# Loading x and two small weights at the start of a fused attention and MLP kernel in another order and from other queues

## The chip, the cores and the metric

The kernel runs on one core of a Trainium2 chip. The metric is device time in microseconds of one execution; the median of three runs before the change is 721.4 us (720.83 to 721.46). One further execution was taken by the profiler; every number of the trace comes from it.

## The reference

The kernel computes a transformer block whose attention and MLP work side by side on the same normalised input, for 2048 tokens of width 512, in bf16. Attention has 32 query heads of 16 channels and one key and value head that all of them share.

```
xn = layernorm(x)                                   # 2048 x 512, no gain, no bias
q  = xn @ wq -> 32 heads of 16;  k = xn @ wk;  v = xn @ wv     # wk, wv: 512 x 16
o  = softmax(q k^T / 4) v ;  A = concat(o) @ wo
B  = gelu_tanh(xn @ w1 + b1) @ w2 + b2              # 1792 hidden
out = x + A + B
```

## The kernel before, in words

**Two parts.** The first 24 us are a prologue: x is loaded, normalised, transposed, and K, V and the first queries are projected. From then to the end runs the attention loop: ScalarE computes exponentials (line 1110), VectorE computes others in integer arithmetic (lines 1141, 1162, 1194) with help of GpSimd (line 1161), TensorE computes scores (line 1086) and the products with V (line 1154), and the query projections, MLP and output products (lines 763 and 767) are put between them.

**Order.** All instructions are recorded through `add`, each with what it reads and writes, and a list scheduler (`schedule`) then fixes each engine's order for good; `emit` adds the semaphore waits. At run time each engine executes its own list in order. In the prologue the order of the engines' instructions follows the table `PRO_DUE`, that of DMAs their own due numbers.

**Tiles and pieces.** x has 16 row tiles of 128 rows by 512 (128 KB each), loaded as eight pieces: piece i holds tiles 2i and 2i+1 (256 KB, two rows of 1 KB on each of 128 partitions). Lines 775 to 778 issue them: piece 1 from ScalarE's queue, piece 0 and then 2 to 7 from SyncE's. Lines 779 and 780 issue wk and wv (16 KB each, in rows of 32 bytes) from ScalarE's queue behind piece 1; lines 781 to 783 issue wq, w1 and w2 from SyncE's queue behind piece 7. wo follows (line 1035). Each DMA has a semaphore of its own; whoever reads the data first waits for that.

**Normalising.** `ln_batch` takes the statistics of a tile. For 14 tiles VectorE does this: bn_stats (line 858) and bn_aggr (line 872). For tiles 1 and 4 ScalarE does it in two passes over the tile: a sum (line 855) and, after GpSimd has made the negative mean (line 861), a sum of squares (line 865). ScalarE makes the reciprocal deviation by Ln and Exp (lines 877 and 879). `normed` scales the tile on GpSimd or VectorE (line 895) or ScalarE (line 891), `x_T` transposes it on TensorE (line 914) and copies it back (lines 919 and 921). VectorE takes the tiles' statistics in the order 0, 5, 2, 7, 3, 8, 12, 9, 15, 6, 13, 10, 14, 11, that is the pieces in the order 0, 2, 1, 3, 4, 6, 7, 5. The first use of wk is a copy on GpSimd (line 810), that of wv the V projection on TensorE (line 743, `wvk` as an operand), and that of wq a copy on GpSimd (line 985). TensorE's products with zeros (line 1522) are fillers that keep it busy.

Of the kernel before, what the change touches and what calls it, by code (L numbers as in the profile page):

```python
# [10 lines left out]
P = 128  # L11
# [106 lines left out]
TBW = 512  # L118
# [495 lines left out]
def bass_parallel_sum__grouped_kv_mqa__dense_activation_gelu__prompt_kernel(  # L614
# [33 lines left out]
    with ExitStack() as es:  # L648
# [82 lines left out]
        def dve(fn, r=(), w=(), n=TBW, mode=1, allow=1.0, **kw):  # L731
            return add("dve", fn, r, w, occ=vcost(n, mode), lat=dlat[0], allow=allow, **kw)

        def act(fn, r=(), w=(), n=TBW, allow=0.0, lat=0.22, **kw):
            return add("act", fn, r, w, occ=0.051 + n / 1.2e3, lat=lat, allow=allow, **kw)
# [35 lines left out]
        def dma(eng, o, i, stream, r=(), w=(), lat=2.2, allow=1.0, **kw):  # L771
            return add(eng, lambda e: e.dma_start(o, i), r, w, dma=stream, occ=0.7, lat=lat, allow=allow, **kw)
# [8 lines left out]
        dma("sp", wq_sb[:], A_wq.rearrange("(k p) n -> p k n", p=P), "d_wq", w=["wq"], due=0.4, lat=9.4)  # L781
        dma("sp", w1_sb[:], B_w1.rearrange("(k p) n -> p k n", p=P), "d_w1", w=["w1"], due=0.5, lat=10.4)
        dma("sp", w2_sb[:], B_w2.rearrange("(k p) n -> p k n", p=P), "d_w2", w=["w2"], due=0.7, lat=16.4)
# [57 lines left out]
        def land(ti):  # L841
            return LAND[ti // 2] + 0.2 * (ti % 2)

        col, batch_of = {}, {}

        def ln_batch(ts, how):
            c0, n = len(col), len(ts)
# [4 lines left out]
            for ti in ts:  # L852
                c = col[ti]
                if how == "a":
                    act(lambda e, ti=ti, c=c: e.activation(scr, x_sb[:, ti, :], ACT.Identity, accum_out=sm[:, c:c + 1]),
                        r=[("x", ti)], w=["scr", ("sm", ti)], n=TBW + 320, lat=0.3)
                else:
                    dve(lambda e, ti=ti, c=c: e.bn_stats(stats[:, c, :], x_sb[:, ti, :]), r=[("x", ti)], w=[("st", ti)],  # L858
                        n=511)
# [133 lines left out]
        for _, _, kind, a in sorted(steps, key=lambda s: s[:2]):  # L993
            if kind == "ln":
                ln_batch(list(a[0]), a[1])
            elif kind == "tr":
                x_T(list(range(*a[0])), a[1], a[2])
            elif kind == "k":
                k_proj(list(range(*a[0])), a[1])
            elif kind == "v":  # L1000
                v_tiles(range(*a))
                if a[1] in (NVA, NT):
                    k_max(0 if a[1] == NVA else NVA, a[1])
            else:
# [559 lines left out]
```

## Time and profile before

| what | us |
|---|---|
| median of three runs | 721.4 (720.83 to 721.46) |
| profiled execution, its own time | 720.62 |
| its span, first to last instruction | 718.8 |
| outside the span | 1.8 |
| first exponential of the loop starts (ScalarE, line 1110) | 24.42 |
| busy share of the span: PE, ACT, DVE, POOL | 98%, 98%, 97%, 63% |

PE is TensorE, ACT ScalarE, DVE VectorE, POOL GpSimd, SP SyncE. Times inside the profile count from the start of the span. A DMA appears twice: as the instruction that issues it on its engine's sequencer (SPq, ACTq), and as time to landing, from the start of that instruction to the last signal of its semaphore. q1 is the queue of SyncE's DMAs, q10 that of ScalarE's; both run on the same 16 DMA engines.

### The profile page before, as it was taken

To read this page: it belongs to the slowest core of one execution; us is meant where nothing else is said; L and a number is where in the kernel's file an instruction comes from. 1 tells how busy PE (TensorE), PEld (TensorE's weight loads), DVE (VectorE), ACT (ScalarE), POOL (GpSimd) and SP (SyncE) were. 2 spreads that over 40 slices of the span, in tenths; PEclk is the share of its full clock that TensorE was granted. 3 is DMA by queue.
4 is the path that set the end of the run, shared out by engine and by line. 5 is a ranking of instruction groups with operands and counts; after the bars stand their busy time and mean duration, and the time that the engine had idled before them with its cause. 6 is when DMAs were issued, how large, how long until landed. Compare 5 with 4: busy or idle time off the path is not lost.

```text
span 718.8 us, 22616 instructions
## 1 busy us (share of the span) xinstructions
PE 704.6 (98%) x9221; PEld 219.2 (30%) x9224; DVE 699.1 (97%) x1387; ACT 703.8 (98%) x762; POOL 452.2 (63%) x739
## 2 busy tenths in 40 slices
PE   7999999999999999999999999999999999999998
PEld 5332232222243333223222232222233222222233
DVE  8899999999999999999999999999999999999986
ACT  7899999999999999999999999999999999999997
POOL 8456557786733446787777636676775786767531
PEclk9999999999999999999999999999999999999999
DMA  9200100101010010010101110100100111101111
GB/s 307 81 10 17 33 10 11 32 16 26 9 41 25 24 33 17 14 28 22 39 7 26 47 40 17 29 17 15 24 18 17 25 32 18 39 21 28 27 30 41
DMA packets 36254, 23.59 MB, mean 33 GB/s; under 512 B 17768, under 2 KB 32568, under 8 KB 36152
## 3 DMA queue, kind: packets, MB, share of 16 engines
q1 hardware_dynamic: 34824, 21.86, 12.1%
q8 instruction: 74, 1.21, 0.7%
q10 hardware_dynamic: 1328, 0.30, 0.2%
q14 instruction: 28, 0.23, 0.1%
HBM read 13.28 MB, written 2.35 MB: 22 GB/s over the span
## 4 chain that ended last, share of the span: by engine, by line
ACT 52%; PE 42%; DVE 5%; DMA 1%; issue 0%; SPq 0%
ACT E L1110 49%; PE pAll L1154 21%; PE pAll L1086 13%; PE pAll L767 6%; PE pAll L749 2%; DVE Dt L1141 2%; ACT ub L1343 1%; DVE stats L858 1%; ACT x_sb L1348 1%; DMA x_sb<-in_A_x_dram 1%; DVE Dt L1194 1%; DVE Dt L1162 0%; PE pAll L914 0%; ACT x_sb L1343 0%; PE pAll L1522 0%
## 5 line engine op out<-in xcount | busy, mean ns | idle before, releaser
L1110 ACT ACTIVATE E<-pAll 128x1024 bf16<-128x1024 f32 (+2 forms) x676 | 652.2, 1146 | 2.9 <-PE pAll L1086 1.2
L1161 POOL INT64_ADD Dt<-Dt x671 | 429.9, 649 | 246.0 <-DVE Dt L1141 79.6
L1141 DVE TENSOR_SCALAR Dt<-pAll 128x512 int16<-128x512 f32 (+1 forms) x599 | 412.5, 706 | 6.5 <-PE pAll L763 4.4
L1154 PE MATMUL pAll<-Dt,V 128*32 128x512 bf16 x3120 | 417.1, 383 | 0.0
L1154 PE MATMUL pAll<-E,V 128*32 128x512 bf16 x1424 | 284.5, 385 | 0.5 <-DVE Of L1240 0.4
L1086 PE MATMUL pAll<-QT,KT 32*128 32x512 bf16 x2048 | 266.7, 384 | 5.5 <-ACT E L1110 4.2
L1194 DVE TENSOR_SCALAR Dt<-Dt 128x1024 int16<-128x1024 int16 (+7 forms) x291 | 160.9, 563 | 2.2 <-PE pAll L1154 1.9
L1086 PEld LDWEIGHTS pAll<-QT,KT 32*128 32x128 bf16 x2048 | 66.5, 90 | 276.5 <-ACT E L1110 260.9
L1154 PEld LDWEIGHTS pAll<-Dt,V 128*32 128x32 bf16 x3120 | 106.8, 94 | 115.4 <-issue 79.5
L1162 DVE TENSOR_SCALAR Dt<-Dt 128x1024 int16<-128x1024 int16 (+1 forms) x270 | 90.0, 360 | 0.1
L1154 PEld LDWEIGHTS pAll<-E,V 128*32 128x32 bf16 x1424 | 65.7, 94 | 49.1 <-issue 38.5
L767 PE MATMUL pAll<-xnT,w_sb 128*32 128x512 bf16 x520 | 70.5, 382 | 0.0
L767 PE MATMUL pAll<-w_sb,ub 128*32 128x512 bf16 x364 | 49.4, 381 | 0.0
L763 PE MATMUL pAll<-w_sb,x_sb 32*128 32x512 bf16 x116 | 44.6, 384 | 0.1
L767 PE MATMUL pAll<-w_sb,x_sb 128*32 128x512 bf16 x276 | 42.1, 382 | 0.0
L763 PE MATMUL pAll<-xnT,w_sb 32*128 32x512 bf16 x88 | 33.8, 384 | 0.0
L763 PE MATMUL pAll<-w_sb,ub 32*128 32x512 bf16 x84 | 32.3, 384 | 0.0
L767 PE MATMUL pAll<-wop,oTp 128*32 128x512 bf16 x192 | 29.4, 382 | 0.0
L767 PEld LDWEIGHTS pAll<-xnT,w_sb 128*32 128x32 bf16 x520 | 18.2, 95 | 10.9 <-issue 5.2
L763 PE MATMUL pAll<-xnT,wq_sb 32*128 32x512 bf16 x56 | 21.5, 384 | 0.0
L767 PE MATMUL pAll<-xnT,wq_sb 128*32 128x512 bf16 x200 | 20.7, 383 | 0.2
L1320 DVE TENSOR_SCALAR ub<-pAll,b1T 128x512 bf16<-128x512 f32 x28 | 20.8, 744 | 0.0
(135 smaller groups left out, 357.9 us busy)
## 6 DMA issues: line engine op xcount, KB each, us to landing
w_sb<-in_B_w_dram SPq DMA_DIRECT2D x2, 1792.0 KB, 13.9
OfP<-Of SPq DMA_DIRECT2D x96, 32.0 KB, 2.0
rbP<-rden_rows SPq DMA_DIRECT2D x96, 32.0 KB, 1.9
x_sb<-in_A_x_dram SPq DMA_DIRECT2D x16, 128.0 KB, 2.2
QT<-qp SPq DMA_DIRECT2D x124, 16.0 KB, 1.8
out_dram<-x_sb SPq DMA_DIRECT2D x15, 128.0 KB, 1.7
x_sb<-in_A_x_dram SPq DMA_DIRECT2D x7, 256.0 KB, 5.3
OfP<-Of SPq DMA_DIRECT2D x56, 16.0 KB, 1.8
```

Source lines behind the costliest of these rows:

```text
L749: add("pe", lambda e, c=c, j=j: e.matmul(o[c, :], l[:, c], rh, start=start, stop=stop, tile_position=(0, 32 * j)), r, [(k, j) for k in w] ...
L763: add("pe", lambda e, b, c=c, j=j: e.matmul(pM, l[c, :], rh[c, :], start=False, stop=b, skip_group_check=True, tile_position=(32 * j, 0)), ...
L767: add("pe", lambda e, b, c=c, j=j: e.matmul(pM[c, :], l[:, c], rh, start=n == 0, stop=b, skip_group_check=True, tile_position=(0, 32 * j)) ...
L858: dve(lambda e, ti=ti, c=c: e.bn_stats(stats[:, c, :], x_sb[:, ti, :]), r=[("x", ti)], w=[("st", ti)], n=511)
L1086: ins = e.matmul(o, l, rh, start=True, stop=True, tile_position=(q0, 0))
L1110: o = act(lambda e: e.activation(E[:, s0:s0 + na, :], bank(b0, na).rearrange("p (a n) -> p a n", a=na), ACT.Exp, scale=LN2 / 128.0), w=[B( ...
L1141: op = dve(lambda e: e.tensor_scalar(Dt[:, s:s + n, :], bank(bk, n).rearrange("p (a n) -> p a n", a=n), float(127 * 128) + SPL_D, SPL_MIN, ...
L1154: add("pe", lambda e, a, b: e.matmul(pO[32 * j:32 * j + 32, :], V1[:, v, kt, :], rhs, start=a, stop=b, tile_position=(0, 32 * j)), r=r + [ ...
L1161: return e.int64_add(d.bitcast(dt.uint64), x.bitcast(dt.uint64), k * 0x0001000100010001 % 2 ** 64)
L1162: return e.tensor_scalar(d, x, float(k), None, ALU.add)
L1194: dve(lambda e, d=view(o, nb), q=view(i, nb), k=k: e.tensor_scalar(d, q, float(k), None, ALU.add), r=keys(i), w=keys(o), n=nb * n * TBW, m ...
L1320: dve(lambda e: e.tensor_scalar(ubs[tb % 2][:, ft, :], pM, b1T[:, ft:ft + 1], None, ALU.add), r=["b1T"], w=M4 + [ukey(tb, ft)], n=TBW + 57 ...
```

## The change

Four edits, all in the prologue's loads; the tables and the code of the loop stay as they are.

1. Piece 0 is issued as two DMAs of one tile each, with a semaphore each (`d_xf0`, `d_xf1`). The readers of tile 0 wait for the first, those of tile 1 for the second.
2. ScalarE's queue loads piece 2 where it loaded piece 1.
3. SyncE's queue loads the rest in the order 1, 3, 4, 6, 7, 5, so it issues eight DMAs of x where it issued seven.
4. wv is issued from ScalarE behind its first pass over tile 1 (line 855), not right behind wk.

`X_LAT`, `occ` and `lat` are estimates that the scheduler alone reads.

```
-X_Q = "sassssss"
-X_LAT = (3.1, 3.3, 3.5, 3.6, 3.7, 3.8, 3.8, 3.8)
+X_FIRST = (0, 1)
+X_SEQ = (1, 3, 4, 6, 7, 5)
+X_LAT = {1: 3.2, 2: 2.9, 3: 2.9, 4: 3.0, 6: 3.8, 7: 3.8, 5: 1.7}
...
-        for i in range(8):
-            e = X_Q[i]
-            dma("sp" if e == "s" else "act", x_sb[:, 2 * i:2 * i + 2, :], x_view[:, 2 * i:2 * i + 2, :], f"d_x{i}",
+        for ti in X_FIRST:
+            dma("sp", x_sb[:, ti, :], x_view[:, ti, :], f"d_xf{ti}", w=[("x", ti)], lat=3.1 if ti == X_FIRST[0] else 2.4, due=0.0)
+        for i in (2,) + X_SEQ:
+            dma("act" if i == 2 else "sp", x_sb[:, 2 * i:2 * i + 2, :], x_view[:, 2 * i:2 * i + 2, :], f"d_x{i}",
                 w=[("x", 2 * i), ("x", 2 * i + 1)], lat=X_LAT[i], due=0.0)
...
-        dma("act", wvk[:, :, 0:Dh], A_wv.rearrange("(k p) n -> p k n", p=P), "d_wv", w=["wv_s"], due=0.2, lat=5.9)
+        wvd = dma("act", wvk[:, :, 0:Dh], A_wv.rearrange("(k p) n -> p k n", p=P), "d_wv", w=["wv_s"], due=0.2, occ=0.01, lat=4.75)
...
-                    act(lambda e, ti=ti, c=c: e.activation(scr, x_sb[:, ti, :], ACT.Identity, accum_out=sm[:, c:c + 1]),
-                        r=[("x", ti)], w=["scr", ("sm", ti)], n=TBW + 320, lat=0.3)
+                    late_w.append(act(lambda e, ti=ti, c=c: e.activation(scr, x_sb[:, ti, :], ACT.Identity, accum_out=sm[:, c:c + 1]),
+                        r=[("x", ti)], w=["scr", ("sm", ti)], n=TBW + 320, lat=0.3))
...
+        wvd.sdeps.append((late_w[0], False))
```

On ScalarE, at the start of the program, these stood before the change (x_sb is x, wvk holds wv and wk, the first ACTIVATE is the sum over tile 1):

```order
L838 ACT_TABLE_LOAD
L772 DMA x_sb<-in_A_x_dram 128x2x512
L772 DMA wvk<-in_A_wk_dram 128x4x16
L772 DMA wvk<-in_A_wv_dram 128x4x16
L855 ACTIVATE oTp,sm<-x_sb 128x512 [waits tk_d_x0]
L877 ACTIVATE lnv<-mv,epsc 128x1 [waits tk_dve,tk_pool]
L865 ACTIVATE oTp,sm<-x_sb,nm 128x512 [waits tk_pool]
L879 ACTIVATE rstd<-lnv 128x1 [waits tk_act]
L855 ACTIVATE oTp,sm<-x_sb 128x512 [waits tk_d_x2,tk_act]
```

On the same engine and at the same place after the change (the file has grown by a line or two, so that the line numbers are higher):

```order
L840 ACT_TABLE_LOAD
L773 DMA x_sb<-in_A_x_dram 128x2x512
L773 DMA wvk<-in_A_wk_dram 128x4x16
L857 ACTIVATE oTp,sm<-x_sb 128x512 [waits tk_d_xf1]
L773 DMA wvk<-in_A_wv_dram 128x4x16
L879 ACTIVATE lnv<-mv,epsc 128x1 [waits tk_dve,tk_pool]
L867 ACTIVATE oTp,sm<-x_sb,nm 128x512 [waits tk_pool]
L881 ACTIVATE rstd<-lnv 128x1 [waits tk_act]
L857 ACTIVATE oTp,sm<-x_sb 128x512 [waits tk_d_x2,tk_act]
```

The issue of wv has moved behind the sum over tile 1, and that sum waits for tile 1 alone. On SyncE, at the start of the program, before:

```order
L772 DMA x_sb<-in_A_x_dram 128x2x512 x7
L772 DMA wq_sb<-in_A_wq_dram 128x4x512
L772 DMA w1_sb<-in_B_w1_dram 128x4x1792
L772 DMA w2_sb<-in_B_w2_dram 128x14x512
L772 DMA wop<-in_A_wo_dram 128x4x512
```

On SyncE at the same place, after:

```order
L773 DMA x_sb<-in_A_x_dram 128x512 x2
L773 DMA x_sb<-in_A_x_dram 128x2x512 x6
L773 DMA wq_sb<-in_A_wq_dram 128x4x512
L773 DMA w1_sb<-in_B_w1_dram 128x4x1792
L773 DMA w2_sb<-in_B_w2_dram 128x14x512
L773 DMA wop<-in_A_wo_dram 128x4x512
```

One issue more stands ahead of wq. TensorE and GpSimd have the same rows as before throughout, line numbers aside, and on VectorE nothing differs but the semaphore for which the first bn_stats waits.

More of the change, by code (lines that the diff above doesn't have):

```diff
@@ L769, in chunk, with dma @@
                         r, M4[j:j + 1] if n == 0 else (), kind="side", tag=(None, j), chain=M4[j] if n else None, **kw)
-        def dma(eng, o, i, stream, r=(), w=(), lat=2.2, allow=1.0, **kw):
-            return add(eng, lambda e: e.dma_start(o, i), r, w, dma=stream, occ=0.7, lat=lat, allow=allow, **kw)
+        def dma(eng, o, i, stream, r=(), w=(), occ=0.7, lat=2.2, allow=1.0, **kw):
+            return add(eng, lambda e: e.dma_start(o, i), r, w, dma=stream, occ=occ, lat=lat, allow=allow, **kw)
         x_view = xf.rearrange("(t p) d -> p t d", p=P)
-        for i in range(8):
-            e = X_Q[i]
-            dma("sp" if e == "s" else "act", x_sb[:, 2 * i:2 * i + 2, :], x_view[:, 2 * i:2 * i + 2, :], f"d_x{i}",
+        for ti in X_FIRST:
+            dma("sp", x_sb[:, ti, :], x_view[:, ti, :], f"d_xf{ti}", w=[("x", ti)], lat=3.1 if ti == X_FIRST[0] else 2.4, due=0.0)
+        for i in (2,) + X_SEQ:
+            dma("act" if i == 2 else "sp", x_sb[:, 2 * i:2 * i + 2, :], x_view[:, 2 * i:2 * i + 2, :], f"d_x{i}",
                 w=[("x", 2 * i), ("x", 2 * i + 1)], lat=X_LAT[i], due=0.0)
         dma("act", wvk[:, :, Dh:2 * Dh], A_wk.rearrange("(k p) n -> p k n", p=P), "d_wk", w=["wk_s"], due=0.1, lat=5.9)
-        dma("act", wvk[:, :, 0:Dh], A_wv.rearrange("(k p) n -> p k n", p=P), "d_wv", w=["wv_s"], due=0.2, lat=5.9)
-        dma("sp", wq_sb[:], A_wq.rearrange("(k p) n -> p k n", p=P), "d_wq", w=["wq"], due=0.4, lat=9.4)
-        dma("sp", w1_sb[:], B_w1.rearrange("(k p) n -> p k n", p=P), "d_w1", w=["w1"], due=0.5, lat=10.4)
-        dma("sp", w2_sb[:], B_w2.rearrange("(k p) n -> p k n", p=P), "d_w2", w=["w2"], due=0.7, lat=16.4)
+        wvd = dma("act", wvk[:, :, 0:Dh], A_wv.rearrange("(k p) n -> p k n", p=P), "d_wv", w=["wv_s"], due=0.2, occ=0.01, lat=4.75)
+        dma("sp", wq_sb[:], A_wq.rearrange("(k p) n -> p k n", p=P), "d_wq", w=["wq"], due=0.4, lat=8.7)
+        dma("sp", w1_sb[:], B_w1.rearrange("(k p) n -> p k n", p=P), "d_w1", w=["w1"], due=0.5, lat=9.7)
+        dma("sp", w2_sb[:], B_w2.rearrange("(k p) n -> p k n", p=P), "d_w2", w=["w2"], due=0.7, lat=15.7)
         def setup(fn, r=(), w=(), occ=0.16, due=0.0, lat=0.1, **kw):
@@ L842, in land @@
             return LAND[ti // 2] + 0.2 * (ti % 2)
-        col, batch_of = {}, {}
+        col, batch_of, late_w = {}, {}, []
         def ln_batch(ts, how):
```

## The prediction

> **What bounds the kernel now.** I read the page first: busy time of the engines, then the chain of work that ended last.
>
> ```profile
> PE 704.6 (98%) x9221; PEld 219.2 (30%) x9224; DVE 699.1 (97%) x1387; ACT 703.8 (98%) x762; POOL 452.2 (63%) x739
> ACT 52%; PE 42%; DVE 5%; DMA 1%; issue 0%; SPq 0%
> ```
>
> The loop keeps three engines 97 to 98% busy, and loads make 1% of the chain. The change touches no instruction of the loop and none of its order, so it can only move the moment at which the loop starts. I therefore asked for the chain in the first 40 us (start, length, what):
>
> ```profile
> 1.31 4.37 DMA x_sb<-in_A_x_dram
> ...
> 5.71 1.29 DVE stats L858 x2
> 7.00 0.08 DVE mv L872
> 7.08 0.58 DVE stats L858
> ...
> 9.48 1.04 PE pAll L914 x8
> 10.52 1.28 PE pAll L1522 x6
> ...
> 24.42 7.44 ACT E L1110 x8
> ```
>
> The chain starts with the piece of x that was issued at 1.31, SyncE's second, which is piece 2. From its landing it runs through VectorE's statistics up to the scaling of a tile, then through the transposes at 9.48, and alternates between VectorE, TensorE and ScalarE until the first exponential at 24.42. So the start of the loop hangs on piece 2, and what VectorE waits for behind it is what matters. VectorE's own rows, with the waits for DMA in brackets:
>
> ```profile
> 4.47 0.69 DVE L858 BATCH_NORM_STATS2 stats<-x_sb 128x6 f32<-128x512 bf16 x1 [1.67 <-DMA x_sb<-in_A_x_dram]
> 5.20 0.18 DVE L872 BATCH_NORM_AGGREGATE mv<-stats 128x2 f32<-128x6 f32 x1
> 5.71 1.29 DVE L858 BATCH_NORM_STATS2 stats<-x_sb 128x6 f32<-128x512 bf16 x2 [0.32 <-DMA x_sb<-in_A_x_dram]
> 6.91 0.17 DVE L872 BATCH_NORM_AGGREGATE mv<-stats 128x2 f32<-128x6 f32 x1
> 6.99 0.66 DVE L858 BATCH_NORM_STATS2 stats<-x_sb 128x6 f32<-128x512 bf16 x1
> 8.90 0.53 DVE L895 TENSOR_SCALAR ub<-x_sb,nm,rstd 128x512 bf16<-128x512 bf16 x1
> ```
>
> The rows are tile 0 (4.47), tiles 5 and 2 (5.71 and about 6.32), tile 7 (6.99) and the scaling of tile 1 (8.90). Behind 5.71 nothing there waits for a load any more.
>
> **When the pieces land.** The issues, and the times to landing, each from an answer for the issues that ran in one narrow stretch; SyncE's are its first, second, third, fourth and seventh (pieces 0, 2, 3, 4, 7), then ScalarE's piece 1, wk and wv:
>
> ```profile
> 0.80 3.54 SPq L772 DMA_DIRECT2D x_sb<-in_A_x_dram  x7
> 0.82 0.48 ACTq L772 DMA_DIRECT2D x_sb<-in_A_x_dram  x1
> 1.34 0.49 ACTq L772 DMA_DIRECT2D wvk<-in_A_wk_dram  x1
> 1.85 0.53 ACTq L772 DMA_DIRECT2D wvk<-in_A_wv_dram  x1
> ...
> x_sb<-in_A_x_dram SPq DMA_DIRECT2D x1, 256.0 KB, 3.7
> x_sb<-in_A_x_dram SPq DMA_DIRECT2D x1, 256.0 KB, 4.4
> x_sb<-in_A_x_dram SPq DMA_DIRECT2D x1, 256.0 KB, 5.0
> x_sb<-in_A_x_dram SPq DMA_DIRECT2D x1, 256.0 KB, 5.3
> x_sb<-in_A_x_dram SPq DMA_DIRECT2D x1, 256.0 KB, 6.0
> ...
> x_sb<-in_A_x_dram ACTq DMA_DIRECT2D x1, 256.0 KB, 3.9
> wvk<-in_A_wk_dram ACTq DMA_DIRECT2D x1, 16.0 KB, 4.5
> wvk<-in_A_wv_dram ACTq DMA_DIRECT2D x1, 16.0 KB, 5.1
> ```
>
> SyncE's seven issues are 3.54/7 = 0.51 apart, so landings are: piece 0 at 0.8+3.7 = 4.5, piece 1 at 0.8+3.9 = 4.7, piece 2 at 1.3+4.4 = 5.7, piece 3 at 1.8+5.0 = 6.8, piece 4 at 2.3+5.3 = 7.6, piece 7 at 3.9+6.0 = 9.9, wk at 5.8, wv at 7.0. From piece 4 to piece 7 that is 2.3 for three pieces, 0.75 each; from piece 2 to piece 3 it is 1.1. What else moved then is in the packet counts (queue, packets, MB, share), for 1.8 to 2.9, for 1.8 to 3.7, and for 5.2 to 6.3:
>
> ```profile
> q1 hardware_dynamic: 122, 0.12, 72.6%
> ...
> q1 hardware_dynamic: 257, 0.25, 62.4%
> ...
> q10 hardware_dynamic: 527, 0.02, 27.3%
> ```
>
> SyncE's queue had moved half of its first piece by 2.9 and all of it by 3.7. Between 5.2 and 6.3, while piece 3 was on its way, the 512 small packets of wv took 27% of the DMA engines' time, 0.3 of the 1.1 us.
>
> **The change part by part.** *Piece 0 in two.* Its first half should land 3.7−2.9 = 0.8 earlier, at 3.7, the second half where the whole landed, 4.5. Tile 0's statistics then run from 3.7 (VectorE is idle for 1.67 before 4.47, so from 2.8), and its bn_aggr ends 5.38−4.47 = 0.9 later, at 4.6. ScalarE's sum over tile 1 starts at 4.5 as before. By itself this gains nothing: VectorE would only wait longer for piece 2. The eighth issue costs SyncE 0.51; it delays wq, which has cover (below).
>
> *Piece 2 for piece 1 on ScalarE's queue.* It stands where piece 1 stood, same size and same neighbours: 4.7 instead of 5.7. Piece 1 takes the place of piece 2 as the bytes 256 to 512 KB of SyncE's queue, behind the same total: 5.7. Its issue is 0.5 later (two ahead of it), 1.8 instead of 1.3, but the queue ahead of it is busy until 3.7, so its own turn decides, not its issue. Tile 5 thus starts at 4.75 (was 5.71). Tile 2 could start 0.61 later, at 5.36, but now waits for piece 1: 5.7 (was 6.32). Gain so far 0.6.
>
> *wv moved.* Tile 7 could start 6.99−6.32 = 0.67 behind tile 2, at 6.37 to 6.4. It needs piece 3, third of SyncE's queue as before. Without wv's packets it lands 0.75 behind piece 1, at 6.45; with the old spacing of 1.1, at 6.8. I take 6.45, since wv is the only traffic that leaves and the pace of 0.75 is measured where no small packets ran; bounds 6.4 and 6.8. Tile 7 starts at 6.5 instead of 6.99: **0.45 to 0.5 gained**; by the bounds 0.6 and 0.17.
>
> *The rest of x.* Tile 8 follows tile 7 by two bn_stats and a bn_aggr, 0.58+0.08+0.58, so at 7.75; piece 4 lands by 7.6 at the latest. Pieces 6 and 7 each gain one place (0.75) because 5 goes last. VectorE wants 6 behind the scaling of tile 1, at 8.42+0.53 = 8.95, and 7 two bn_stats later, past 10; 7 lands near 9.1 even with wv among them. Piece 5, last at 9.9, is first read by tile 10, three tiles behind tile 15, so not before 12. The scaling of tile 1 and all behind it follow, if ScalarE delivers:
>
> ```profile
> 4.47 0.63 ACT L855 ACTIVATE oTp<-x_sb 128x512 bf16<-128x512 bf16 x1 [2.40 <-DMA x_sb<-in_A_x_dram]
> 5.49 0.29 ACT L877 ACTIVATE lnv<-mv,epsc 128x1 f32<-128x1 f32 x1 [0.29 <-DVE mv L872]
> 6.39 0.19 ACT L879 ACTIVATE rstd<-lnv 128x1 f32<-128x1 f32 x1
> 7.97 0.33 ACT L879 ACTIVATE rstd<-lnv 128x1 f32<-128x1 f32 x2
> ...
> 7.11 0.77 POOL L895 TENSOR_SCALAR ub<-x_sb,nm,rstd 128x512 bf16<-128x512 bf16 x1
> ```
>
> *The issue of wv on ScalarE* takes 0.53 and stands between the sum over tile 1 (4.47 to 5.2 with its read-out) and the Ln at 5.49; everything on ScalarE is queued behind it. Bounds: nothing, when it runs beside the sum as the issues at 0.82 to 2.4 run beside the table load; or 5.2+0.53 = 5.73, 0.24 late. At worst the deviation of tile 0 ends at 6.82 instead of 6.58, and GpSimd takes it at 7.11, so 0.53 of cover hides it. The deviations of tiles 1 and 2 (7.97 to 8.3) follow the bn_aggr of tile 2, which comes 0.45 earlier; even 0.24 late on ScalarE's side, they come by 8.1, and VectorE wants tile 1's at 8.42. So I cost this issue at nothing; without the cover it would be 0.24.
>
> *wq, w1 and w2* are issued 0.5 later, behind the same bytes.
>
> ```profile
> 15.99 0.40 POOL L985 COPY oTp<-wq_sb 128x256 bf16<-128x256 bf16 x1
> ...
> w_sb<-in_B_w_dram SPq DMA_DIRECT2D x1, 1792.0 KB, 11.0
> ```
>
> wq is as large as two pieces, so it follows x by 1.5, at 11.4, and is copied at 16. w1, issued at 4.9 before, landed 11.0 later, at 15.9, and is read in the loop alone, as w2 is. Nothing.
>
> *Propagation.* From 8.4 on the chain is that of before, made of waits of engines for each other and no landing, so it moves as a whole. One reservation is TensorE's rate, by the rows of its transposes:
>
> ```profile
> 9.48 1.04 PE L914 MATMUL pAll<-ident,ub 128*128 128x128 bf16 x8 [0.30 <-DVE ub L895]
> 15.14 0.55 PE L914 MATMUL pAll<-ident,ub 128*128 128x128 bf16 x7
> ```
>
> Eight take 1.04 at 9.48, seven 0.55 at 15.14, which is 0.63 for eight: TensorE is slower at first and switches in between. If the switch keeps its absolute time, a little more of the work falls before it: 0.45 of shift at a rate lower by two fifths could cost 0.18 if all of it were TensorE's chain. But at 9.48 TensorE had waited 0.30 for VectorE, so it isn't the whole chain; I take off 0.05 at most.
>
> **Sum.** 0.45 to 0.5, less up to 0.05: 0.45 us. The first exponential moves from 24.42 to about 23.97. The profiled execution would go from 720.62 to 720.2. That execution is 0.8 below the median of the runs, 721.4, so the runs go to **720.9**.
>
> [...]
>
> **The rivals.** *Piece 3 stays late* (0.17). If wk's packets or the start of the queues made the 1.1, piece 3 lands at 6.8, tile 7 starts at 6.82, gain 0.17: 721.2. For it: piece 3 and wk overlap too. Against: wk has landed at 5.8.
>
> *The change doesn't shorten the prologue* (0.08): VectorE is early, but GpSimd or ScalarE sets the pace: 721.4. Against: the chain goes through VectorE up to the scaling at 8.90, and TensorE waits for that.
>
> *The rate of TensorE switches at another time* (0.15, half each way). In this execution the switch lies between 9.5 and 15. If it comes only behind the transposes of tiles 4 to 9, three groups of eight at 1.04 instead of 0.63 cost 1.2; if it comes before 9.48, the group there (0.4) and the fillers at 10.52 (1.28, half of it) save about 1.0. That gives 722.1 or 719.9. The kernel before has this too: its runs spread over 0.6. [...]
>
> *Slower: wv comes too late* (0.06). TensorE's V projection stands in the list before the transposes of tiles 4 and 5:
>
> ```profile
> 12.45 0.26 PE L743 MATMUL pAll<-wvk,xnT 128*128 128x32 bf16 x2
> ```
>
> After the change that is 12.0. wv is issued at about 5.1; with the 5.1 that it took before (3.4 of them behind piece 1 and wk) it lands at 10.2 at the latest, and more likely at 8. If ScalarE's queue got its turn only behind SyncE's backlog, behind wq (11.4) would still do; behind w1 it would come at 15.9 and hold up the whole prologue by 3.9: 721.4−0.45+3.9 = 724.9. It decides from a landing after 12.0. Against: from 5.2 to 6.3 q10 got its packets through beside a full q1.
>
> **How the numbers follow.** Forecast (gain 0.3 to 0.6) 0.54, and the rivals 0.17, 0.08, 0.15 and 0.06. Likeliest: 720.9. The range runs from the early switch (719.9) to the late one (722.1), which takes in both bounds of piece 3 and leaves out wv's rival and tails. 0.2% is 1.4 us, about what a measurement of this kernel can tell from no change. Faster by more (under 720.0) needs the gain and an early switch: 0.08. Slower by more (over 722.8) is wv's rival and a little of the late switch: 0.07. Within: 0.85.
>
> **What would show it.** In the profile after: tile 5's bn_stats near 4.75, tile 2's near 5.7, tile 7's near 6.5, the scaling of tile 1 near 8.4, the first exponential near 23.95, and the length from there to the end unchanged. Piece 3 at 6.8 would speak for the first rival; a wait for wv on TensorE for the last; a chain that starts in GpSimd or ScalarE for the second. If the loop itself changes its length, my premise is wrong.

## The result, and the profile after

The changed kernel takes **722.26 us** (median of 15 runs, 721.36 to 724.46) against 720.79 for the kernel before (15 runs beside it, 720.44 to 721.47): a ratio of 1.0022, interval 1.0015 to 1.0030. It is slower by 1.5 us, where 0.45 less had been forecast. Its profiled execution took 723.46 us, 2.84 more than that of before; the first exponential starts at 27.27 instead of 24.42, 2.85 later, and from there to the end both take 696.2. So all of that lies in the prologue, as foreseen, but with the other sign. The profiled execution is the third slowest of the fifteen, 1.2 above their median, so its 2.85 is more than the usual loss; what makes the executions differ by that much is not shown. The one profiled execution of e2 (below) ran at a lower granted clock and took 900.08 us, and no number here rests on it. Line numbers are one to three higher than before (L860 for L858, L897 for L895, L916 for L914, L744 for L743).

The chain of waits of the changed kernel in the first 30 us (start, length, what) has a new member:

```profile
1.25 3.52 DMA x_sb<-in_A_x_dram
4.77 0.02 issue
4.80 9.36 DMA wvk<-in_A_wv_dram
14.16 0.14 issue
14.30 0.21 PE pAll L744 x2
...
27.27 1.02 ACT E L1113
```

It runs from the second half of piece 0 (issued at 1.25) to wv, which is issued at 4.80 and lands 9.36 later, at 14.16, and from there to the V projection. Of these 9.36 us, 3.85 pass before wv's first packet and 5.51 from there to the landing; in the kernel before, the 5.11 were 3.34 and 1.77. So it is above all the moving of the packets that has become long. VectorE's own rows (start, length, and in brackets the idle time ahead with its releaser) show what the prediction said of them:

```profile
3.47 0.69 DVE L860 BATCH_NORM_STATS2 stats<-x_sb 128x6 f32<-128x512 bf16 x1 [0.66 <-DMA x_sb<-in_A_x_dram]
4.30 0.66 DVE L860 BATCH_NORM_STATS2 stats<-x_sb 128x6 f32<-128x512 bf16 x1
5.62 0.69 DVE L860 BATCH_NORM_STATS2 stats<-x_sb 128x6 f32<-128x512 bf16 x1 [0.66 <-DMA x_sb<-in_A_x_dram]
6.37 0.69 DVE L860 BATCH_NORM_STATS2 stats<-x_sb 128x6 f32<-128x512 bf16 x1
8.31 0.39 DVE L897 TENSOR_SCALAR ub<-x_sb,nm,rstd 128x512 bf16<-128x512 bf16 x1
...
14.98 0.41 DVE L897 TENSOR_SCALAR ub<-x_sb,mv,rstd 128x512 bf16<-128x512 bf16 x1 [2.05 <-PE pAll L916]
```

Tiles 0, 5, 2 and 7 start at 3.47, 4.30, 5.62 and 6.37, tile 1 is scaled at 8.31, 0.59 earlier than before. Then VectorE stands still for 2.05, waiting for TensorE. The other engines say why the 0.59 had no effect even ahead of that. ScalarE, GpSimd and TensorE after the change:

```profile
4.79 0.63 ACT L857 ACTIVATE oTp<-x_sb 128x512 bf16<-128x512 bf16 x1 [2.72 <-DMA x_sb<-in_A_x_dram]
4.80 0.42 ACTq L773 DMA_DIRECT2D wvk<-in_A_wv_dram  x1
...
5.61 0.27 POOL L863 TENSOR_SCALAR nm<-sm 128x1 f32<-128x1 f32 x1 [0.72 <-ACT oTp L857]
7.42 0.76 POOL L897 TENSOR_SCALAR ub<-x_sb,nm,rstd 128x512 bf16<-128x512 bf16 x1
8.94 0.76 POOL L897 TENSOR_SCALAR ub<-x_sb,nm,rstd 128x512 bf16<-128x512 bf16 x1
...
9.75 0.93 PE L916 MATMUL pAll<-ident,ub 128*128 128x128 bf16 x7 [0.16 <-POOL ub L897]
```

The same places on GpSimd before:

```profile
5.29 0.27 POOL L861 TENSOR_SCALAR nm<-sm 128x1 f32<-128x1 f32 x1 [0.38 <-ACT oTp L855]
...
8.52 0.76 POOL L895 TENSOR_SCALAR ub<-x_sb,nm,rstd 128x512 bf16<-128x512 bf16 x1
```

Tile 1 lands at 4.77 (4.45 before, in one piece with tile 0), so ScalarE's sum starts at 4.79 instead of 4.47 and GpSimd's negative mean at 5.61 instead of 5.29. Between that and its scaling of tile 0 GpSimd has a list of small instructions without a gap (5.61 to 7.42), so the scalings move along: 7.42 (7.11 before) and 8.94 (8.52). The second group of transposes, which waited for VectorE at 9.48 before, now waits for GpSimd at 9.75.

Last, TensorE's granted clock in stretches (each row has the stretch and its length, the busy time of PE, PEld, DVE, ACT and POOL, then the clock as a share of full speed, the share of the DMA engines and GB/s):

```profile
4.30:7.70 3.40, 0.48 (x4) 0.19 (x2) 2.74 (x8) 2.69 (x10) 2.48 (x15) 1.00 1.08 344
7.70:17.90 10.20, 7.80 (x58) 5.55 (x60) 8.13 (x23) 6.32 (x25) 7.97 (x29) 0.50 1.08 365
17.90:27.30 9.40, 8.64 (x115) 5.41 (x114) 7.73 (x24) 6.37 (x20) 5.53 (x8) 1.00 0.46 143
```

The trace records steps of the clock from the first one on. In the kernel before, the first is a step to full rate at 12.93, so the 1.00 that its rows of this kind read ahead of that (from 9.50 to 12.90, for one) is no measurement; the eight transposes at 9.48 take 1.04 there, as eight do in h3 at a granted clock of 0.50 (1.03 at 9.40), where g2 has them in 0.62 at full rate (9.50). Here there is a step up at 4.28, one down at 7.69 and one up at 17.93, five us later than before.

### The profile page after: what moved, and what is told of

Its sections match the earlier page's. It is cut to its first block, busy times and chain, and to the rows that moved or that the text cites. A ratio compares the mean times of both kernels' runs of the same rounds, so it can differ in the third digit from the quotient of the medians.

```text
span 721.6 us, 22617 instructions
## 1 busy us (share of the span) xinstructions
PE 705.3 (98%) x9221; PEld 220.0 (30%) x9224; DVE 699.7 (97%) x1387; ACT 703.8 (98%) x762; POOL 451.0 (62%) x739
## 4 chain that ended last, share of the span: by engine, by line
ACT 52%; PE 42%; DVE 4%; DMA 2%; issue 0%; SPq 0%
ACT E L1113 49%; PE pAll L1157 21%; PE pAll L1089 13%; PE pAll L768 6%; PE pAll L750 2%; DVE Dt L1144 2%; DMA wvk<-in_A_wv_dram 1%; ACT ub L1346 1%; ACT x_sb L1351 1%; PE pAll L744 1%; DVE Dt L1197 1%; DMA x_sb<-in_A_x_dram 0%; PE pAll L916 0%; DVE Dt L1165 0%; ACT x_sb L1346 0%
```

## The experiments

Three theories. **Turns**: wv is late because each of its small packets waits for a packet of SyncE's queue, and those become long when w1 starts. **GpSimd**: the prologue's pace is set by tile 1's landing, ScalarE's sum and GpSimd's list, and not by VectorE, so the claimed gain can't show. **Clock**: TensorE's idle time keeps its rate at half for longer, which is a loss of its own, on top of the wait. The rival to the first is that wv is late because it is issued late; to the second that VectorE's chain decides, as the prediction had it. In every kernel the engines keep the order of the kernel before, but for the loads and what the edit names.

What the profiles show, ordered by loads (us; "full from": where TensorE's rate goes to full and stays so through the prologue; the ratio comes from the runs of both kernels and need not be that of their medians):

| run | loads | ratio to before (95% interval) | piece 3 lands | wv lands | full from | first exponential |
|---|---|---|---|---|---|---|
| before | old | 1 | 6.75 | 6.96 | 12.93 | 24.42 |
| h3_wv_late_again | old, wv late | 1.0002 (0.9993 to 1.0010) | 6.52 | 10.93 | 11.49 | 24.08 |
| h1_gpsimd_alone | old, GpSimd's list short | 1.0003 (0.9994 to 1.0012) | 6.69 | 7.59 | 14.16 | 24.66 |
| g2_warm_before | old, more fillers | 1.0004 (0.9995 to 1.0013) | 6.84 | 7.04 | 6.22 | 24.64 |
| after | the change | 1.0022 (1.0015 to 1.0030) | 6.34 | 14.16 | 17.93 | 27.27 |
| f4_wv_big_rows | the change | 1.0026 (1.0015 to 1.0036) | 6.48 | 14.04 | 17.29 | 27.00 |
| f3_fill_wait | the change, fillers in the wait | 1.0017 (1.0008 to 1.0027) | 6.99 | 13.78 | 13.55 | 26.09 |
| g1_wv_rows_of_128 | the change, wv in 128 packets | 1.0002 (0.9993 to 1.0011) | 6.48 | 10.90 | 11.45 | 24.23 |
| e3_w1_small_rows | the change, w1 in rows of 1 KB | 1.0004 (0.9995 to 1.0013) | 6.64 | 11.93 | 12.03 | 24.52 |
| f1_wv_on_sync | edits 1 to 3, wv on SyncE | 1.0006 (0.9997 to 1.0015) | 6.97 | 10.35 | 13.39 | 24.76 |
| e1_wv_behind_wk | edits 1 to 3 | 1.0004 (0.9995 to 1.0013) | 6.81 | 6.20 | 13.86 | 24.68 |
| i1_whole_wv_on_sync | edits 2, 3, wv on SyncE | 0.9996 (0.9987 to 1.0005) | 6.67 | 10.04 | 11.16 | 23.93 |
| i2_whole_wv_late | edits 2, 3, 4 | 0.9996 (0.9988 to 1.0005) | 6.58 | 11.52 | 12.57 | 24.27 |
| h2_whole_piece_0 | as i1, GpSimd's list short | 0.9996 (0.9987 to 1.0004) | 6.51 | 9.90 | 13.16 | 24.09 |
| h4_gpsimd_order_again | as f1, GpSimd's list short | 0.9996 (0.9987 to 1.0006) | 6.56 | 9.97 | 13.34 | 24.24 |
| f2_gpsimd_order | the same kernel as h4 | 1.0005 (0.9996 to 1.0014) | 7.59 | 11.00 | 14.93 | 25.37 |
| g4_gpsimd_wv_early | edits 1 to 3, GpSimd's list short | 1.0005 (0.9996 to 1.0014) | 7.91 | 6.28 | 13.37 | 25.30 |
| g3_gpsimd_warm | as f2, more fillers | 1.0002 (0.9993 to 1.0011) | 7.71 | 11.10 | 4.68 | 25.30 |
| e4_halves_two_queues | halves on two queues | 1.0004 (0.9995 to 1.0013) | 7.55 | 10.34 | 16.05 | 25.81 |

### Is it wv?

**Edits 1 to 3 without edit 4** (e1): wv is issued right behind wk.

```
-        wvd = dma("act", wvk[:, :, 0:Dh], ..., "d_wv", occ=0.01, lat=4.75)
+        dma("act", wvk[:, :, 0:Dh], ..., "d_wv", lat=5.9)
-        wvd.sdeps.append((late_w[0], False))
```

> Edits 1 to 3 without edit 4: wv goes back to its place behind wk. Theory W (the late wv is the loss): wv lands near 6 to 7, the V projection no longer waits for it (14.30 in the changed kernel), and the time falls by about 1.5 from the changed kernel's 722.26, to the kernel before's or below it. Theory G (GpSimd's list of small operations, started by the sum over tile 1, sets the pace; tile 1 landed 0.3 later): the time ends level with the kernel before or 0.1 to 0.3 above, not below, with the V projection at 12.5 to 12.8. My prediction's own steps without wv's rival would give 0.2 to 0.45 below the kernel before. Theory R (the loss is TensorE's slower rate, set by the phase of its clock, not by wv): the time stays near 722.3.

The loss is gone: 720.94 against 720.72. But no gain has come in its place, and the chain shows why, starting with the second half of piece 0:

```profile
1.25 3.63 DMA x_sb<-in_A_x_dram
...
5.44 0.20 ACT oTp L857
5.72 0.27 POOL nm L863
...
7.55 0.75 POOL ub L897
...
8.96 0.85 POOL ub L897
9.86 0.93 PE pAll L916 x7
```

VectorE isn't in it up to the transposes at 9.86; the path is tile 1, ScalarE's sum, and GpSimd's list.

**Edit 4 alone** (e2, and h3 once more): the old loads, wv behind the sum over tile 1.

```
         # X_Q and the loop of the kernel before
+        wvd = dma("act", wvk[:, :, 0:Dh], ...)      # behind late_w[0], as in the change
```

> The kernel before with edit 4 alone; pieces of x as before. W: wv is issued at about 4.5, lands at 13.5 to 14.5, the V projection waits from 12.45 on, and the time is 1.2 to 2.0 above the kernel before. R or another cause among edits 1 to 3: within 0.3 of the kernel before.

> Edit 4 alone, as in the second experiment, for a profile at full clock. Turns theory: wv lands between 12.4 and 14.2 as with the changed loads, since w1 starts at the same time, TensorE waits up to 1.5 us; then the median must lie above that of before by as much as the wait, 0.3 to 1.3. The earlier median (720.77, no loss) speaks for a landing at 12.6 or before.

e2 gave 720.77 against 720.72 (ratio 1.0000, 0.9991 to 1.0009). h3, the same kernel, gave 720.71 against 720.72, with wv landing at 10.93 and no wait. So edit 4 alone costs nothing, against what was expected. The likely reason is that wv was issued at 4.33 there, not at 4.80, and its first packet started at 8.24, not at 8.65.

**w1 in rows of 1 KB** (e3): the changed kernel, w1 in four DMAs by columns.

```
-        dma("sp", w1_sb[:], B_w1.rearrange(...), "d_w1", w=["w1"])
+        for i, (c0, c1) in enumerate(((0, 512), (512, 1024), (1024, 1536), (1536, 1792))):
+            dma("sp", w1_sb[:, :, c0:c1], w1_view[:, :, c0:c1], "d_w1", ...)
```

> The changed kernel with w1 loaded as four DMAs of 1 KB (the last 512 B) rows instead of one with rows of 3.5 KB; wv stays late. W with turns (a small packet of wv waits for one packet of the other queue on each engine, so its pace follows the size of those packets): wv starts near 8.5 as in the changed kernel, moves at the pace it had beside 1 KB packets (130 in 0.5 us), and lands near 10.5 to 11.5, before it is needed; time about that of e1. If wv is late because its descriptors stand behind a backlog, whatever the size of the packets beside it, it lands near 14 again and the time stays near 722.3.

wv, issued at 4.85 like in the change, lands at 11.93 instead of 14.16, and 720.96 against 720.72 is left of the loss.

**wv in 128 packets** (f4, then g1): the changed kernel, wv read in rows of 128 bytes (its rows end up in another order, so V is another one).

```
-wvk[:, :, 0:Dh], A_wv.rearrange("(k p) n -> p k n", p=P)
+wvk[:, 0],       A_wv.rearrange("(p k) n -> p k n", p=P)     # wvk as [P, 2, DT, Dh]; f4 without this layout
```

> The changed kernel, with wv read in 128 rows of 128 bytes instead of 512 of 32 bytes: same bytes, queue and moment of issue. The rows of wv then stand in another order, so V and with it the output are not the reference's; the time of the rest is the same. Turns theory: each packet of wv waits a turn of SyncE's queue, so a quarter of the packets needs about a quarter of the turns: first packet at 8.6 as before, last near 10, landing at 10 to 11 instead of 14.2; TensorE doesn't wait and the time is 720.7 to 721.0. If the size of wv's packets doesn't matter (the late first packet or the backlog of bytes decides), it lands at 13 to 14 and the time stays at 722.3.

> The changed kernel with wv's place in SBUF laid out so that one partition's share of wv is one row of 128 bytes at both ends: 128 packets instead of 512, same bytes, same queue, same moment of issue. The rows of wv then stand in another order, so the output is not the reference's; the work is the same. (The run before it was meant to do this, but its rows in SBUF were still 32 bytes, and it still moved 512 packets.) Turns theory: with a quarter of the packets, last packet near 10 and landing at 10 to 11 instead of 14.2, no wait on TensorE, 720.7 to 721.1. If the number of packets doesn't matter, landing at 13.5 to 14.2 and 722.0 to 722.9 as in the changed kernel.

f4 still moved 512 packets of 32 bytes, because its rows in SBUF had stayed that short: it repeats the change, with the same loss (722.95 against 720.71). g1 moved 128. Issue to landing of wv in f4 and in g1:

```profile
wvk<-in_A_wv_dram ACTq DMA_DIRECT2D x1, 16.0 KB, 9.2
```

```profile
wvk<-in_A_wv_dram ACTq DMA_DIRECT2D x1, 16.0 KB, 6.0
```

Same bytes, same queue, issue at 4.86 and 4.89: 3.2 us less by the number of packets alone, and 721.01 against 720.65.

**wv on SyncE's queue** (f1): issued at 4.76, between piece 5 and wq.

```
-        wvd = dma("act", wvk[:, :, 0:Dh], ..., "d_wv", ...)     # behind late_w[0]
+        dma("sp", wvk[:, :, 0:Dh], ..., "d_wv", due=0.3)         # ahead of wq
```

> The changed kernel, but wv is issued from SyncE's queue, between the last piece of x and wq, so that w1 can't run ahead of it. Turns theory: wv's packets stand in the same queue ahead of wq's and w1's, so it lands about 1 us behind piece 5, near 10.5, TensorE does not wait for it (its V projection needs it at about 12.4), and the time falls from 722.3 to 720.7 to 721.0. If the delay of wv came from its being issued late and not from w1's packets, it lands at 14 or later again (it is issued at about the same time, 4.5) and the time stays at 722.3. GpSimd theory: piece 3 lands at 6.3 and VectorE is 0.5 early, but tile 1 lands at 4.8, GpSimd takes the first tile at 7.4 or later, and the first exponential is not before 24.4: no gain over the kernel before (720.8). The prediction's theory (VectorE's tiles decide) gives 720.3.

```profile
wvk<-in_A_wv_dram SPq DMA_DIRECT2D x1, 16.0 KB, 5.6
```

It lands at 10.35 (issued as late as in the change), TensorE doesn't wait, 721.01 against 720.71. So a late issue alone doesn't cost; being overtaken by w1 does. As in e1, no gain.

**The change without edit 1** (i2): piece 0 whole.

```
-        for ti in X_FIRST:
-            dma("sp", x_sb[:, ti, :], x_view[:, ti, :], f"d_xf{ti}", ...)
-        for i in (2,) + X_SEQ:
+        for i in (2, 0) + X_SEQ:
```

> The change without edit 1: piece 0 whole, wv issued from ScalarE behind the sum over tile 1. The sum starts at 4.4 to 4.5, so wv is issued at 4.3 to 4.4 instead of 4.8; its first packet follows 3.9 to 4.1 later, at 8.3, and most of its packets pass while SyncE's queue still moves packets of 1 KB: landing at 10.5 to 12.4, no wait on TensorE, first exponential at 24.1 to 24.3, median 720.5 to 720.8. If wv is late by the order of the loads and not by those 0.4 us, it lands at 13.5 to 14.2, and the median is 721.5 to 722.3.

720.52 against 720.89: no loss. wv is issued at 4.37, 0.43 earlier than in the change, since tile 1 is there earlier, and lands at 11.52, 2.64 earlier. Packets (queue, packets, MB, share of the DMA engines) from 8.5 to 10.5 and from 10.5 to 12.5, in i2:

```profile
q1 hardware_dynamic: 603, 0.61, 101.6%
q10 hardware_dynamic: 502, 0.02, 20.1%
...
q1 hardware_dynamic: 249, 0.78, 103.6%
q10 hardware_dynamic: 26, 0.00, 1.0%
```

The same in the changed kernel:

```profile
q1 hardware_dynamic: 592, 0.66, 106.4%
q10 hardware_dynamic: 352, 0.01, 13.7%
...
q1 hardware_dynamic: 212, 0.76, 99.0%
q10 hardware_dynamic: 159, 0.00, 4.7%
```

In i2 all but 26 of the 528 packets that wv makes on q10 (512 of data, 16 signals) have started by 10.5, while SyncE's packets are of 1 KB (603 take 101.6% of 16 engines for 2 us, 0.054 us each). In the change 160 of the 512 are left when w1's packets of 3.5 KB have begun (212 take 99.0%, 0.15 us each), and from 10.5 to 12.5 q10 starts 159 beside those 212, 0.75 for each. That is a cliff: a difference of some tenths of a us became 2.64 of landing. Where these tenths come from is less plain than the issue suggests. wv's first packet starts at 8.65 in the change and at 8.67 in i2, at the same moment. But from 8.5 to 9.5 q10 moves 112 packets in the change and 228 in i2, and w1's first packet starts at 9.98 instead of 10.15. i2 doesn't separate these two. These rows fit the turns, with 502 beside 603 and 159 beside 212; how a DMA engine chooses between the two queues they don't show. It is otherwise between 5.2 and 6.3 of the kernel before, where q10 moved 527 packets (its row stands in the prediction) beside these:

```profile
q1 hardware_dynamic: 294, 0.28, 93.3%
```

That is nearly two for one, and why was not found.

### Where did the gain go?

**GpSimd's list shortened** (f2, and the same kernel again as h4): as f1, and the constants between the negative mean and the scalings moved: four ahead, into idle time, the others behind the copy of wq and the squares of the first queries.

```
+    for o in early + late + mid:
+        v.remove(o)                 # v: GpSimd's list; i: the negative mean of tile 1
+    v[i:i] = early                  # mrow, mask4 twice, h05
+    v[j:j] = mid                    # mask4, selr: behind the copy of wq
+    v[k:k] = late                   # V1 five times, hbi, kcst: behind sqq
```

> As f1, and GpSimd's small constants (eleven instructions of 0.1 to 0.2 us) no longer stand between the negative mean of tile 1 and the scaling of tiles 0 and 2: four run ahead of it in GpSimd's idle time, the rest behind the copy of wq and behind the squares of the first queries, where GpSimd idles. GpSimd theory: it takes the scaling of tile 0 at about 6.7 (7.4 in the changed kernel) and that of tile 2 at about 8.2 to 8.4 (8.94), so the 0.5 that VectorE had gained comes through: first exponential at 23.9 to 24.1, 0.4 less than f1, 720.3 to 720.5. If GpSimd isn't what held it, the same as f1 within 0.2. If the place to which the constants have moved is worse, later than f1: then GpSimd's rows at 20 to 22 show whom they hold up.

> The GpSimd run (piece 0 in two, wv on SyncE's queue, constants out of the way) once more, unchanged. If a DMA engine that falls behind is chance from execution to execution, this profile may be without it: then piece 3 lands at 6.4, scaling of tile 1 at 8.3 to 8.4, first exponential at 23.9 to 24.1. If it belongs to these loads, piece 3 lands at 7 to 8 again, first exponential at 25.3. Median 720.9 to 721.4 either way, as before.

f2 missed: 721.37 against 720.71. GpSimd scaled tile 0 at 6.89 as expected, but VectorE was held up:

```profile
7.62 0.70 DVE L904 BATCH_NORM_STATS2 stats<-x_sb 128x6 f32<-128x512 bf16 x1 [1.19 <-DMA x_sb<-in_A_x_dram]
```

Tile 7 waits 1.19 for piece 3. That piece's semaphore had fifteen of its sixteen signals by 6.36; the last came at 7.59, and every later piece has one late signal (a straggler) by as much. h4, the same kernel, has it not: piece 3 at 6.56, first exponential at 24.24, 720.58 against 720.72. So the straggler is of the execution, not of the kernel. Of h4's 11 runs one lies above 721, of f2's six: two medians of one kernel are 0.8 apart, and a single difference of that size between two kernels would show little.

**The same with wv behind wk** (g4: e1 with GpSimd's new order):

> Edits 1 to 3 with wv right behind wk (as the first experiment) and GpSimd's constants out of the way. GpSimd theory: in the first experiment the chain ran from tile 1's landing over GpSimd's list to the transposes at 9.86; now it runs over VectorE again, whose third piece lands at 6.8: scaling of tile 1 at 8.8, transposes of the second group at 9.3 to 9.4, first exponential at 24.2 to 24.4 where the first experiment had 24.68, median 720.4 to 720.8. If GpSimd didn't hold it: the transposes at 9.8 and the first exponential at 24.6 to 24.7 again.

Inconclusive in the profile, for the same reason: fifteen signals of piece 3 by 6.77, the last at 7.91. 721.52 against 720.65.

**The loads of before with GpSimd's new order** (h1):

> The loads of before, GpSimd's constants out of the way. If VectorE's chain (pieces 2, 1 and 3) decides with the loads of before, as the chain of the kernel before shows, GpSimd's scalings come 0.4 to 0.6 earlier and nothing else moves: scaling of tile 1 at 8.9, first exponential at 24.3 to 24.5, median 720.6 to 720.8. All landings within 0.5 us over the 16 engines. If GpSimd's new order costs something, first exponential at 24.6 or later.

Tile 1 is scaled by VectorE at 8.92 as before, GpSimd's tile 0 at 6.89; 720.91 against 720.72, nothing gained. With the old loads VectorE's chain does decide, as the prediction read it.

**Piece 0 whole** (h2: as h4 without edit 1; i1: the same with GpSimd's old order):

```
-        for ti in X_FIRST: ...
-        for i in (2,) + X_SEQ:
+        for i in (2, 0) + X_SEQ:
```

> Edits 2 and 3 without edit 1 (piece 0 is one load again, lands at 4.5), wv on SyncE's queue behind piece 5, GpSimd's constants out of the way. If the split of piece 0 makes a DMA engine late, all landings stay within 0.5 us, tile 5 starts at 5.2 (behind tile 0), tile 7 at 6.5 to 6.6, the first exponential comes at 23.9 to 24.2 and the median is 720.3 to 720.5, the gain that the prediction claimed. If the late engine has nothing to do with the split, piece 3 lands at 7 to 8 here as well and the median is 721.

> Edits 2 and 3 with piece 0 whole and wv on SyncE's queue behind piece 5, GpSimd's order as before. Tile 1 lands at 4.4 again, so the negative mean of tile 1 is at 5.2 to 5.3 and GpSimd scales tile 0 at 7.1 and tile 2 at 8.5, as before; VectorE scales tile 1 at 8.5, 0.4 earlier. Then GpSimd's scaling of tile 2 (ends at 9.25) is what the second group of transposes waits for: 9.3 instead of 9.48, first exponential at 24.1 to 24.3, a gain of 0.1 to 0.3, median 720.5 to 720.7. If GpSimd doesn't matter once tile 1 is on time, 23.95 and 720.3; if it takes the whole gain, 24.4 and 720.7.

h2 gives 720.56 (720.41 to 720.65) against 720.72, the first exponential 0.33 earlier; i1 gives 720.55 against 720.89. Where the second group of transposes starts and for whom it waits, in h2 and in i1:

```profile
9.13 1.03 PE L958 MATMUL pAll<-ident,ub 128*128 128x128 bf16 x8 [0.16 <-DVE ub L939]
```

```profile
9.54 0.71 PE L917 MATMUL pAll<-ident,ub 128*128 128x128 bf16 x5 [0.18 <-POOL ub L898]
```

With GpSimd's list short the group waits for VectorE, at 9.13 (9.48 before): the gain that the prediction claimed. With the old list it waits for GpSimd, at 9.54, and nothing of VectorE's 0.27 (8.63 instead of 8.90) comes through there; by the estimate below, i1's first exponential at 23.93 is owed mostly to TensorE's rate, which is full from 11.16. Part of the 0.41 between the two is that piece 0 landed at 4.37 in h2 and at 4.52 in i1; in i2, with the old list and piece 0 at 4.34, the group starts at 9.35. With piece 0 in two, the same comparison gives 9.29 behind VectorE (h4) and 9.93 behind GpSimd (f1). The medians of h2 and i1 both lie below that of before, within their intervals.

**Halves on two queues** (e4): tile 0 from SyncE, tile 1 from ScalarE, piece 2 and wk behind it, wv on SyncE ahead of piece 5.

> Tile 0 from SyncE's queue and tile 1 from ScalarE's at the same time, piece 2 and wk behind tile 1; wv on SyncE's queue ahead of piece 5. Both theories W and G: tile 1 lands near 4.0 instead of 4.45 (before) and 4.77 (changed), GpSimd's list starts 0.4 to 0.5 earlier than before, wv lands near 9.2, the first exponential comes 0.3 to 0.6 before that of the kernel before, so 720.2 to 720.5. If GpSimd's start doesn't matter, it gains no more than e1 does.

Tile 1 landed at 3.48 and the negative mean came at 4.89, 0.4 earlier than before, but piece 3's last signal came at 7.55, 1.15 behind the fifteenth: 720.97 against 720.72. Inconclusive.

### TensorE's rate

**Fillers in the wait** (f3): the changed kernel, seven more products with zeros ahead of the V projection.

```
+    zero_fill(pr, lists["pe"], at, 7)      # at: the first product that waits for wv
```

> The changed kernel with seven more products with zeros on TensorE ahead of its wait for wv (1.5 us at half rate), so that TensorE isn't idle while it waits; wv is left as late as it was. Clock theory: of the 2.85 us by which the first exponential of the profiled run was late, 1.5 is the wait and the rest is TensorE's half rate until 17.9 instead of 12.9, brought on by the idle time. Then the wait stays, the rate rises at about 14.5, the first exponential comes at 25.7 to 26.2 instead of 27.3, and the median falls by 0.4 to 1.0, to 721.3 to 721.9. If the rate doesn't matter or doesn't depend on that idle time, 722.3 and a first exponential at 27.3; if the fillers themselves hold up the V projection, later than that.

In the profile the first exponential comes at 26.09 as expected, 1.18 earlier; wv landed only 0.38 earlier (13.78). The rate is full from 13.55. But the median is 722.25 against 720.71, no better than the change. The profiled execution, 723.67 us, shows 3.4 us at half rate in the loop, which the change's profile has not:

```profile
13.50:27.20 13.70, 12.20 (x154) 7.17 (x152) 11.99 (x34) 9.53 (x30) 8.98 (x16) 1.00 0.67 223
27.20:30.60 3.40, 3.40 (x25) 0.61 (x25) 1.86 (x3) 2.58 (x3) 1.18 (x3) 0.50 0.03 6
```

From the first exponential to the end it takes 697.6 instead of 696.2. So the rate's loss is there in the prologue, and in this execution what the fillers won was paid again; whether the other eight paid it too is not shown.

**More fillers** (g2 with the loads of before, g3 with f2's):

```
+    for at, n in ((44, 3), (38, 5), (24, 6), (17, 20)):     # g3: 3 for the 6
+        zero_fill(pr, lists["pe"], at, n)
```

> The kernel before, with its loads untouched, and more products with zeros on TensorE in the prologue: 20 more behind the first 17, then 6, 5 and 3 more behind the next three groups. Clock theory: TensorE idles from 5.2 to 7.9 in the kernel before and works at half rate up to 12.9; without the idle time the rate is full from 8.2 at the latest and stays so, the transposes and fillers from 9.5 to 13.1 take half the time, first exponential at 23.3 to 23.9 instead of 24.4, median 719.7 to 720.3. If TensorE isn't the chain there, or the rate stays low, 720.7; if the fillers stand in the way, 721 to 722.

> The run with GpSimd's constants out of the way and wv on SyncE's queue, with more products with zeros on TensorE as well (20, 3, 5 and 3 more). If both theories hold, GpSimd's and the clock's, the gains add: first exponential at 22.9 to 23.5, median 719.3 to 719.9, and less than with the loads of before by 0.4. If a late piece 3 (one DMA engine behind the other 15) is common with eight pieces on SyncE's queue, VectorE holds it up again and it is no better than the same fillers with the loads of before.

Both missed. In g2 the granted clock is full from 6.22 on, but the first exponential comes at 24.64, and 720.88 against 720.65. TensorE is early, but VectorE (third engine in the row of g2 below) is busy for 5.30 of 5.30 us, as it was without the fillers.

```profile
7.70:13.00 5.30, 4.93 (x60) 3.92 (x59) 5.30 (x18) 4.57 (x18) 4.97 (x20) 1.00 1.08 376
```

g3 (720.86 against 720.65) had the straggler, piece 3 at 7.71.

## Why the prediction was wrong

**The step that failed first: wv's landing.** "It lands at 10.2 at the latest, and more likely at 8" took over the 5.1 us that wv had needed before. It needed 9.36, and the V projection started at 14.30, 1.85 later than before. The rival "wv comes too late" named the mechanism's place and its point ("a landing after 12.0") and was given 0.06. It was right, with a landing at 14.16 where it had priced 15.9, though not in the way that it put: wv didn't stand behind SyncE's backlog, its packets moved beside it (352 with 592 from 8.5 to 10.5, 159 with 212 from 10.5 to 12.5). Against it I had held that q10 got its packets through beside a full q1 between 5.2 and 6.3. That is a rate beside packets of 1 KB (294 take 93.3% of 16 engines for 1.1 us, 0.056 us each); behind 10.5 the packets are of 3.5 KB (0.15 us each). e3, g1 and f1 each take one condition away (the long packets, the many packets, the other queue), i2 takes away the 0.43 by which tile 1 and the issue of wv came later, and each takes the loss with it. The kernel of f4, in which none is gone, keeps it.

**The step that put the change over the edge: "the second half where the whole landed, 4.5", "ScalarE's sum over tile 1 starts at 4.5 as before".** The first half megabyte is through at the same time as before (4.77, before 4.75), but its last part is now the second half of piece 0, where it had been piece 1. So tile 1 is 0.3 late, and that does two things: with the old GpSimd list it moves the scalings of tiles 0 and 2 by 0.31 and 0.42, and it makes wv later (issued at 4.80, in i2 at 4.37). Without edit 1 (i2) the other three edits lose nothing. This step doesn't excuse the first one: the prediction had wv issued at 5.1, later still, and forecast a landing by 10.2.

**The step "the scaling of tile 1 and all behind it follow, if ScalarE delivers"** left GpSimd out. The 0.53 of cover that I read at GpSimd's row at 7.11 isn't there: GpSimd had been busy without a gap since 5.29, so that row came when the list was through. The rival "GpSimd or ScalarE sets the pace" (0.08) was right of edits 1 to 3. That is shown by e1's chain, and by h2 against i1 and h4 against f1.

**The rate of TensorE** was given 0.05 at most, as a rival 1.2. Three profiles with the old loads (h3, before, h1) have full rate from 11.49, 12.93 and 14.16 and the first exponential at 24.08, 24.42 and 24.66: about 0.22 us for each us, an estimate from three points, one of them with GpSimd's list short. By that, the changed profile's 2.85 are the V projection's delay of 1.85 (12.45 to 14.30) and some 1.1 for a rate that rises 5.0 later, together 2.95. How much of the 5.0 is the wait's doing is not shown: from 7.69 to 11.10, before TensorE waited for wv, it was busy for 2.70 of 3.41 us, and from 11.10 to 14.52, with the wait, for 1.94 of 3.42, at a granted clock of 0.50 in both. f3's profile, with products in the wait and the rate full from 13.55, supports that the wait has a part in it; in g2 a rise at 6.22 brought nothing more. Put to a rise at 12.93 by the same estimate, the first exponential is at about 24.5 to 24.7 with piece 0 in two (e1, f1, g1), 24.3 with it whole (i1, i2), and 24.05 with GpSimd's list short as well (h2; with piece 0 in two, h4, 24.15). The forecast of 23.97 was thus near the time of another kernel, h2. In medians these gains of some tenths lie within the intervals.

**What held.** Pieces 2, 1 and 3 landed at 4.21, 5.59 and 6.34 and VectorE's tiles and the scaling of tile 1 came as forecast or up to 0.45 earlier; piece 5 last at 9.36, wq at 11.10, w1 at 15.70; the issue of wv on ScalarE ran beside the sum and cost nothing; the loop kept its length. The medians of edits 1 to 3 show no gain (e1, 720.94 against 720.72), but VectorE's rows do show an earlier start: piece 2 landed 1.5 earlier (4.21, 5.7 before), and with h2's GpSimd list that reached the transposes (9.13, 9.48 before).

**What stays open.** In 9 of 19 profiles one or two of the sixteen signals of a load fall 0.4 to 1.3 us behind the others while pieces 3 and 4 are on their way (in f2 fifteen of piece 3's by 6.36, the last at 7.59), and stay so; 7 of these are among the 12 with piece 0 in halves, where it can reach piece 3 (up to 7.91), 2 among the 7 with it whole, where only later pieces had it. Two profiles of one kernel (f2, h4) differ in it. What sets it off wasn't found, nor whether the halves make it likelier.

## What to carry to other kernels

Before a small load is moved later, look at what will share the DMA engines with it *at its new time*: here a load of many small packets moved 0.6 to 1.8 packets for each packet of the other queue (352 beside 592 in the change, 527 beside 294 before), so that its landing depended on the length of those: 14.16 beside w1's rows of 3.5 KB, 11.93 beside rows of 1 KB (e3). Put it into the same queue ahead of the large one (10.35 in f1), or give it fewer, longer rows (10.90 in g1). And where a chain of waits names one engine, read the other engines' lists at the same place too: one that runs without a gap up to the row of interest has no cover, whatever its neighbours show, and takes over the chain as soon as the first one is sped up, as GpSimd did here (busy from 5.29 to 7.11 before; the transposes waited for it at 9.86 in e1).

## What the hardware did that was not expected

- wv's first packet came 3.85 us after its issue (8.65 after 4.80), though ScalarE's queue was empty, and in i2 4.30 after it (8.67 after 4.37); in the kernel before wk's came 2.8 and wv's 3.3 after the issue.
- TensorE's granted clock stepped in the change at 4.28, 7.69 and 17.93, 3.41 and three times 3.41 apart, and in f3 at 13.55, 27.20 and 30.60, four times and once 3.4, at a phase that differs from one profile to the next (full from 11.49 in h3, 12.93 before, 14.16 in h1). In e3, f3 and h3 one such stretch of 3.4 us at the start of the loop is at half rate, and from the first exponential to the end they take 697.5 to 697.6 instead of 696.2.
- In g2 two of VectorE's scalings took 1.22 together where they take 0.72 in h3, with TensorE's rate full in both. These 0.5 are most of the distance between the two first exponentials (24.64 and 24.08), so without them g2 would be level with h3, whose rate is full from 11.49 only. The cause is open.
